# Token weights loaded in squares and turned on VectorE, all left-hand operands 32 bytes lower

## The chip, the core and the metric

The kernel runs on one core of a Trainium2 chip. The metric is the device time of one execution in microseconds (us); the median of three runs of the kernel before is 1181.59 us (1181.41 to 1181.63). TensorE is also called PE here, VectorE DVE, ScalarE ACT, GpSimd POOL, and SyncE SP.

## What is computed

Three blocks follow each other on activations of 4 sequences, 448 tokens and 768 features: sigmoid attention, a block that mixes tokens with a low-rank map and then applies a wide two-layer perceptron, and a block that mixes tokens with two full 448x448 matrices. The change touches how those two matrices (`w_tok_r`, `w_tok_i`) are brought in.

```python
attn = 1 / (1 + exp(-(q @ k.T / sqrt(64) - log(448))))     # 4 x 12 heads
x = heads_side_by_side(attn @ v)                           # 4 x 448 x 768

u  = x + (x.T @ U @ V).T                                   # rank 32
x  = u + relu(u @ w_ch1) @ w_ch2                           # 768 -> 3072 -> 768

theta = x @ w_theta
y = w_tok_r @ (x * cos(theta)) + w_tok_i @ (x * sin(theta))
u = x + y
out = u + relu(u @ w_ch)
```

The weights of the second and third block come as 64-bit floats. The kernel reads each as two 32-bit words and makes of them a rounded high part and a low part (type fp32r). A product is then three matmuls: high by high, high by low and low by high.

## The kernel before

`X` holds the activations, turned (features on the partitions), in SBUF for the whole run. PE's work comes in stages, one after the other: attention (to 163 us), the wide perceptron (163 to 883), projection by `w_theta` and mixing of tokens (883 to 1084), and the last product by `w_ch` (1084 to 1174).

**The wide perceptron.** It runs over 12 slices i of the 3072 inner features and, in each, over the 4 sequences b. `ch1(i, b)` (L674 to L676) makes 36 matmuls of 448 columns into a PSUM tile `g`: the weights are slices of `w1`, the moving operands are `uh` and `ul`, the high and low part of the sequence's activations. ACT then makes `gh` of it (L681) and DVE `gl` (L682). `ch2(i, b)` (L696 to L698) makes 36 matmuls into three PSUM tiles `y`, 12 each; the weights are slices of `w2`, the moving operands `gh` and `gl`. DVE adds each `y` to `X` (L700). The order on PE is `ch1(i, b)`, then `ch2` of the pair before it, then `ch1` of the next pair. `uh` and `ul` of the sequences 0 and 1 lie in a pool `u01` on the right side of SBUF, those of 2 and 3 in `u23` on the left.

**The mixing of tokens.** `mix` (L886 to L888) multiplies weights `zh` and `zl` (left side) by the moving operand `tok` (right side). The projection (L809 to L813) takes `xh` and `xl` (right side) as weights and `th_r` (left side, in the rings of `w1` and `w2`) as the moving operand, in 384 columns. The last stage (L967 to L969) has `wc_r` as weights and `uh`, `ul` as moving operands, all on the left.

**Bringing weights in.** Each piece of weight is a `Conv` with a list of steps: `size` (ACT), `bits`, `top` and `word` (DVE) rebuild 32-bit floats from the two words, then `finish` splits them into high and low. The load of a piece is issued in the `size` step of the piece two places before it in the queue. A table `units`, filled by `place` and `place_extra`, says at which tick (slice i, sequence b, point t) a step is taken: t = 0 is before `ch1(i, b)`, t = 1 between `ch1` and `ch2`, t = 2 to 4 behind each of the three `y` tiles of that `ch2`. The engines keep the order in which the code is written.

The seven pieces of the token weights (`conv_tok`, `tok0` to `tok6`) are made during slices i = 2, 4, 6 (two each) and i = 8 (one), spilled to DRAM as `tok_d` and loaded back together as `tok` in the last slice. They must be turned, since the token index of the sum has to lie on the partitions. Before the change a piece lies as 112 partitions by 4 x 128, and PE turns it by four transposes against an identity into a PSUM tile `tkt` (L265), in the middle of a `ch2`; ACT copies the high part from there (L110), and DVE subtracts it (L119). The pieces of `w_theta` and `w_ch` that are spilled in the same way (`conv_kept`) need no turn.

Of the kernel before, what the change touches and what calls it, by code (L numbers as in the profile page):

```python
# [11 lines left out]
F32 = mybir.dt.float32  # L12
F32R = mybir.dt.float32r
U32 = mybir.dt.uint32
# [5 lines left out]
def f(t):  # L20
    return t.bitcast(F32)
# [3 lines left out]
def tile_kernel(  # L25
# [15 lines left out]
    nc = tc.nc  # L41
    B, H, S, D = q.shape
    DM = H * D
    R = moe_U.shape[1]
    DF = moe_w_ch1.shape[1]
    P = 128
    CP = 112
    NC = S // CP
# [9 lines left out]
    NFULL = S // P  # L58
    NZ = 2 * NFULL + 1
    NS = S // R  # L60
# [22 lines left out]
    cpool = ctx.enter_context(tc.tile_pool(name="cpool", bufs=1))  # L83
# [4 lines left out]
    ident = cpool.tile([P, P], F32, name="ident")  # L88
# [10 lines left out]
    tok_w = (w_tok_r.bitcast(U32), w_tok_i.bitcast(U32))  # L99
# [9 lines left out]
    def hi_act(o, i):  # L109
        nc.scalar.activation(o, i, AF.Copy)  # L110
# [7 lines left out]
    def lo_dve(o, i, h):  # L118
        nc.vector.tensor_sub(o, i, f(h))  # L119
# [50 lines left out]
    def split(o, a, lo):  # L170
        hi_act(o[:, 0], a)
        lo(o[:, 1], a, o[:, 0])
# [66 lines left out]
    def conv_tok(i):  # L239

        n_, o_ = divmod(i, NFULL)
        st = {}

        def dma(s):
            if i < NZ - 1:
                nc.sync.dma_start(
                    out=s.rearrange("p (c s) t -> p c (s t)", c=NC),
                    in_=tok_w[n_][:, 2 * o_ * P:2 * (o_ + 1) * P].rearrange("(c p) w -> p c w", p=CP),
                )
            else:  # L250
                sv = s.rearrange("p (c a s) t -> p c a (s t)", c=NC, a=2)
                for n in range(2):
                    nc.sync.dma_start(
                        out=sv[:, :, n], in_=tok_w[n][:, 2 * NFULL * P:].rearrange("(c p) w -> p c w", p=CP)
                    )

        def dest():
            st["t"] = spill_tile(f"tok{i}")
            st["n"] = st["t"][:CP, 2 * S:2 * S + NC * P]
            return st["n"].bitcast(U32)  # L260

        def turn():
            ps = ps_g.tile([P, 2, 512], F32, tag="g", name=f"tkt_{i}", bufs=2)
            for c in range(NC):
                nc.tensor.transpose(ps[:, 0, c * CP:(c + 1) * CP], st["n"][:, c * P:(c + 1) * P], ident[:CP, :CP])  # L265
            st["o"] = st["t"][:, :2 * S].rearrange("p (a n) -> p a n", a=2)
            o = st["o"].bitcast(F32R)
            hi_act(o[:, 0], ps[:, 0, :S])
            lo_dve(o[:, 1], ps[:, 0, :S], o[:, 0])

        def spill():
            nc.sync.dma_start(out=tok_d[:, :, i, :], in_=st["o"])
        return Conv(f"tok{i}", CP, NC * P, dma, None, False, [turn, spill], dest)

    def conv_U(par):
        def dma(s):
# [94 lines left out]
    kT_t, qT_t = {}, {}  # L371
# [194 lines left out]
    nc.vector.memset(bias_s, NEG_LOG_S)  # L566
    nc.vector.memset(half_pi, math.pi / 2)
    warm = cpool.tile([P, 1], F32, name="warm")
    gate = cpool.tile([P, 1], F32, name="gate")
    load_qk(0)  # L570
    make_identity(nc, ident)
    nc.scalar.activation(warm, bias_s, AF.Sigmoid)
# [35 lines left out]
    for p in range(NP):  # L608
# [4 lines left out]
            TK(p + 1)  # L613
            TQ(p + 1)()
        if p == 0:
            nc.gpsimd.tensor_copy(gate, kT_t[1][:, :1])
            seq[0].load()
            seq[1].load()
        if p:
# [13 lines left out]
        if b >= 0 and r < NK // 2:  # L633
            ps = ps_a.tile([P, 2, 512], F32, tag="ux", name=f"h_{b}_{r}")
# [28 lines left out]
    ps_g, ps_g_st = pool("ps_g", "right", PSUM)  # L663
# [85 lines left out]
    for i in range(NB):  # L749
        for b in range(B):  # L750
# [3 lines left out]
            if i == L and b == 1:  # L754
# [3 lines left out]
                tok = tokhl.tile([P, 2, NZ, S], F32R, name="tok")  # L758
# [32 lines left out]
    ps_t, st = pool("ps_t", "right", PSUM)  # L791
    ctx.enter_context(st)
    ps_e, st = pool("ps_e", "left", PSUM)
    ctx.enter_context(st)
    zp, st = pool("zp")
# [154 lines left out]
    for bi, b in enumerate(turns_):  # L950
        for e2 in range(NK // 2):
# [3 lines left out]
            else:  # L955
                ps = ps_t.tile([P, 2, 512], F32, tag="th", name=f"wc_{b}_{e2}", bufs=2)
# [3 lines left out]
            for e in range(2):  # L960
                m = 2 * e2 + e
                o = ps1[e][:, 0, :S] if final else ps[:, e, :S]
# [42 lines left out]
```

## Time and profile before

| What | Value |
|---|---|
| median of three runs | 1181.59 us |
| the profiled execution | 1180.82 us |
| its span, first to last instruction | 1179.0 us |
| TensorE busy | 1169.3 us, 6442 matmuls |
| VectorE busy | 643.3 us |
| ScalarE busy | 360.5 us |
| GpSimd busy | 176.7 us |
| TensorE's granted clock, mean | 0.999 of 2.4 GHz |
| DMA | 100.57 MB, 85 GB/s on average |

A matmul's recorded duration is longer than the distance to the next one's start, since matmuls overlap. So the starts of matmuls are read, and the lengths of stretches cut at such starts; the durations aren't added up.

### The profile page before, as it was taken

Reading aid. Unit: us, or ns where it says so; the run is one execution under the profiler, and the core shown is the slowest. Engines: PE = TensorE matmul, PEld = TensorE weight load, DVE = VectorE, ACT = ScalarE, POOL = GpSimd, SP = SyncE. Lnnn points to the kernel's source line nnn. Section 1 sums busy time; section 2 is a strip of 40 time slices with the busy share of each in tenths; the row PEclk is TensorE's granted clock in tenths of the full one; section 3 lists DMA queues with packets and bytes.
Section 4 is the critical chain, followed back from the end, with each engine's and each line's share of the span. In section 5 each row is a group of like instructions: output and inputs, shape, how many; then the busy total and the mean of one; then the engine's idle time right before and its main releaser. Section 6 shows DMA issues by size and latency. Waiting matters only on the chain.

```text
span 1179.0 us, 15627 instructions
## 1 busy us (share of the span) xinstructions
PE 1169.3 (99%) x6442; PEld 1003.2 (85%) x6442; DVE 643.3 (55%) x805; ACT 360.5 (31%) x465; POOL 176.7 (15%) x129
## 2 busy tenths in 40 slices
PE   8999999999999999999999999999999999999998
PEld 4444468999999999999999999999999999999997
DVE  5787763455555555555545566565375543732443
ACT  6878753121212121212121212122125341620110
POOL 3200014010101010101010112122002221410000
PEclk9999999999999999999999999999999999999999
DMA  8877700113231223132313232424431000120333
GB/s 181 173 160 157 170 30 1 54 54 96 70 112 54 97 70 112 54 96 69 112 54 97 81 123 69 146 63 152 163 134 54 1 1 1 48 114 1 63 64 63
DMA packets 174439, 100.57 MB, mean 85 GB/s; under 512 B 138368, under 2 KB 165376, under 8 KB 174240
## 3 DMA queue, kind: packets, MB, share of 16 engines
q1 hardware_dynamic: 147520, 87.95, 26.2%
q0 software_dynamic: 2368, 8.24, 2.3%
q10 hardware_dynamic: 24480, 3.39, 1.7%
q8 instruction: 50, 0.82, 0.3%
q14 instruction: 21, 0.17, 0.1%
HBM read 81.40 MB, written 18.15 MB: 84 GB/s over the span
## 4 chain that ended last, share of the span: by engine, by line
PE 99%; ACT 0%; POOL 0%; issue 0%; DVE 0%; POOLq 0%
PE y L696 10%; PE g L674 10%; PE y L697 10%; PE y L698 10%; PE g L675 10%; PE g L676 10%; PE av L428 5%; PE sc L402 4%; PE y L888 3%; PE y L886 3%; PE y L887 3%; PE th L809 3%; PE th L813 3%; PE th L810 2%; PE wc L967 2%; PE wc L969 2%
## 5 line engine op out<-in xcount | busy, mean ns | idle before, releaser
L700 DVE TENSOR_TENSOR X<-y,X 128x896 f32<-128x896 f32 x144 | 157.1, 1091 | 118.8 <-PE y L698 118.7
L696 PE MATMUL y<-gh,w 128*128 128x448 f32 x576 | 212.6, 369 | 0.0
L674 PE MATMUL g<-uh,w 128*128 128x448 f32 x576 | 211.9, 368 | 0.0
L698 PE MATMUL y<-gh,w 128*128 128x448 f32 x576 | 211.8, 368 | 0.0
L697 PE MATMUL y<-gl,w 128*128 128x448 f32 x576 | 211.7, 367 | 0.0
L675 PE MATMUL g<-ul,w 128*128 128x448 f32 x576 | 211.7, 367 | 0.0
L676 PE MATMUL g<-uh,w 128*128 128x448 f32 x576 | 210.7, 366 | 0.0
L681 ACT ACTIVATE gh<-g 128x896 fp32r<-128x896 f32 x48 | 44.2, 920 | 421.5 <-PE g L676 421.5
L682 DVE SCALAR_TENSOR_TENSOR gl<-g,gh 128x896 fp32r<-128x896 f32 x48 | 52.4, 1092 | 195.6 <-ACT gh L681 195.6
L113 POOL TENSOR_TENSOR w<-ca_w,w 128x768 fp32r<-128x768 f32 x42 | 78.0, 1856 | 502.5 <-ACT w L110 502.5
L674 PEld LDWEIGHTS g<-uh,w 128*128 128x128 f32 x576 | 108.0, 187 | 11.8 <-ACT uh L110 0.7
L696 PEld LDWEIGHTS y<-gh,w 128*128 128x128 f32 x576 | 108.1, 188 | 11.4 <-issue 1.0
L698 PEld LDWEIGHTS y<-gh,w 128*128 128x128 f32 x576 | 108.1, 188 | 10.6
L697 PEld LDWEIGHTS y<-gl,w 128*128 128x128 f32 x576 | 108.2, 188 | 10.3
L676 PEld LDWEIGHTS g<-uh,w 128*128 128x128 f32 x576 | 108.2, 188 | 10.1
L675 PEld LDWEIGHTS g<-ul,w 128*128 128x128 f32 x576 | 108.1, 188 | 9.7
L393 ACT ACTIVATE A<-sc,bias_s 128x896 f32<-128x896 f32 x72 | 72.2, 1007 | 23.4 <-PE sc L402 13.2
L428 PE MATMUL av<-A,v 128*64 128x448 f32 x288 | 64.5, 556 | 0.0
L886 PE MATMUL y<-tok,zh 128*128 128x448 f32 x168 | 61.8, 368 | 0.0
L888 PE MATMUL y<-tok,zl 128*128 128x448 f32 x168 | 61.8, 368 | 0.0
L887 PE MATMUL y<-tok,zh 128*128 128x448 f32 x168 | 61.3, 365 | 0.0
L110 ACT ACTIVATE w<-ca_w 128x768 fp32r<-128x768 f32 x48 | 40.3, 840 | 65.3 <-PE y L698 64.8
(140 smaller groups left out, 1628.4 us busy)
## 6 DMA issues: line engine op xcount, KB each, us to landing
ws_w<-in_moe_w_ch_dram SPq DMA_DIRECT2D x40, 768.0 KB, 4.3
ws_w<-in_moe_w_ch_dram POOLq DMA_DIRECT2D x8, 768.0 KB, 5.9
k<-in_k_dram SPq DMA_DIRECT2D x94, 56.0 KB, 2.5
q<-in_q_dram SPq DMA_DIRECT2D x93, 56.0 KB, 2.6
ws_th<-in_moe_w_theta_dram SPq DMA_DIRECT2D x6, 768.0 KB, 4.2
th_d<-sp_th SPq DMA_DIRECT2D x6, 768.0 KB, 4.0
ws_wc<-in_moe_w_ch_dram SPq DMA_DIRECT2D x6, 768.0 KB, 4.9
wc_d<-sp_wc SPq DMA_DIRECT2D x6, 768.0 KB, 3.6
```

The source lines that it names most:

```text
L113: nc.gpsimd.tensor_sub(o, a, b)
L428: nc.tensor.matmul(ps[h * D:(h + 1) * D, :S], v_t[p // 2][:, 2 * (p % 2) + h, c, :], A_t[p, c][:, h, :], start=c == 0 and p % 2 == 0, stop ...
L674: nc.tensor.matmul(o, wh[:, sl], uh_t[b][:, kk, :], start=kk == 0, stop=False)
L675: nc.tensor.matmul(o, wh[:, sl], ul_t[b][:, kk, :], start=False, stop=False)
L676: nc.tensor.matmul(o, wl[:, sl], uh_t[b][:, kk, :], start=False, stop=kk == NK - 1)
L696: nc.tensor.matmul(o, wh[:, sl], gh[:, j, :], start=j == 0, stop=False)
L697: nc.tensor.matmul(o, wh[:, sl], gl[:, j, :], start=False, stop=False)
L698: nc.tensor.matmul(o, wl[:, sl], gh[:, j, :], start=False, stop=j == FB - 1)
L700: nc.vector.tensor_add(x, ps[:, :, :S], x)
L886: nc.tensor.matmul(o, zh[:, sl], tok_h[:, i, :], start=n == 0, stop=False)
L887: nc.tensor.matmul(o, zh[:, sl], tok_l[:, i, :], start=False, stop=False)
L888: nc.tensor.matmul(o, zl[:, sl], tok_h[:, i, :], start=False, stop=n == NZ - 1)
```

## The change

A piece is now loaded as four groups of 32 partitions, one for each group of 32 columns of the matrix, so that each 32x32 square of it lies turned in its place among the squares but not within itself: four DMAs of 32x14x64 words instead of one of 112x4x256 (for the last piece, two from each matrix instead of one from each). DVE's transpose, which works on squares of 32x32, then finishes the turn in one instruction. The piece becomes an ordinary `Conv` with a `finish` step: DVE transposes `ca` into the spill tile, ACT copies the high part, POOL subtracts. PE, the PSUM tile and DVE's subtraction drop out. With a `finish` step the table places `word` behind the last `y` of the sequence before (t = 4) and `finish` at t = 0, and the spill comes at t = 3 instead of 4.

The second edit removes the tile `gate` (128 x 1) and writes the one-column copy that paces the first loads into `warm` instead. A tile of one column takes 32 bytes of each partition. In the built programs the places are, in bytes from the start of a partition:

| Tile | Side | Before | After |
|---|---|---|---|
| `X` | left | 17088 | 17088 |
| `warm` | left | 60096 | 60096 |
| `gate` | left | 60128 | none |
| first of the `w1`/`w2` rings | left | 60160 | 60128 |
| first `gh`, first `gl` | left | 121600, 128768 | 121568, 128736 |
| `uh`, `ul` of sequence 2 | left | 135936, 146688 | 135904, 146656 |
| `uh`, `ul` of sequence 0 | right | 186336, 197088 | 186336, 197088 |
| first `xh`, first `xl` | right | 191968, 198112 | 191968, 198112 |
| `tok` | right | 204256 | 204256 |

All left tiles behind `gate` lie at multiples of 64 before and 32 bytes past one after; so do those of attention, of `z` and of the last stage. The right side isn't moved; its operands lie 32 bytes past a multiple of 64 in both. Lines of a matmul's operand are 512 or 1792 bytes long, both multiples of 64.

```diff
--- before.py
+++ after.py
@@ -239,38 +239,29 @@
     def conv_tok(i):
 
         n_, o_ = divmod(i, NFULL)
+        cols = [(n_, o_ * P + a * R) for a in range(P // R)]
+        if i == NZ - 1:
+            cols = [(a // 2, NFULL * P + a % 2 * R) for a in range(P // R)]
         st = {}
 
         def dma(s):
-            if i < NZ - 1:
+            sv = s.rearrange("p (c j) t -> p c (j t)", c=NS)
+            for a, (n, s0) in enumerate(cols):
                 nc.sync.dma_start(
-                    out=s.rearrange("p (c s) t -> p c (s t)", c=NC),
-                    in_=tok_w[n_][:, 2 * o_ * P:2 * (o_ + 1) * P].rearrange("(c p) w -> p c w", p=CP),
+                    out=sv[a * R:(a + 1) * R],
+                    in_=tok_w[n][:, 2 * s0:2 * (s0 + R)].rearrange("(c i) w -> i c w", i=R),
                 )
-            else:
-                sv = s.rearrange("p (c a s) t -> p c a (s t)", c=NC, a=2)
-                for n in range(2):
-                    nc.sync.dma_start(
-                        out=sv[:, :, n], in_=tok_w[n][:, 2 * NFULL * P:].rearrange("(c p) w -> p c w", p=CP)
-                    )
-
-        def dest():
+
+        def fin(a, t):
             st["t"] = spill_tile(f"tok{i}")
-            st["n"] = st["t"][:CP, 2 * S:2 * S + NC * P]
-            return st["n"].bitcast(U32)
-
-        def turn():
-            ps = ps_g.tile([P, 2, 512], F32, tag="g", name=f"tkt_{i}", bufs=2)
-            for c in range(NC):
-                nc.tensor.transpose(ps[:, 0, c * CP:(c + 1) * CP], st["n"][:, c * P:(c + 1) * P], ident[:CP, :CP])
+            x = st["t"][:, 2 * S:3 * S]
+            nc.vector.transpose(out=x, in_=a)
             st["o"] = st["t"][:, :2 * S].rearrange("p (a n) -> p a n", a=2)
-            o = st["o"].bitcast(F32R)
-            hi_act(o[:, 0], ps[:, 0, :S])
-            lo_dve(o[:, 1], ps[:, 0, :S], o[:, 0])
+            split(st["o"].bitcast(F32R), x, lo_pool)
 
         def spill():
             nc.sync.dma_start(out=tok_d[:, :, i, :], in_=st["o"])
-        return Conv(f"tok{i}", CP, NC * P, dma, None, False, [turn, spill], dest)
+        return Conv(f"tok{i}", P, S, dma, fin, False, [spill])
 
     def conv_U(par):
         def dma(s):
@@ -566,7 +557,6 @@
     nc.vector.memset(bias_s, NEG_LOG_S)
     nc.vector.memset(half_pi, math.pi / 2)
     warm = cpool.tile([P, 1], F32, name="warm")
-    gate = cpool.tile([P, 1], F32, name="gate")
     load_qk(0)
     make_identity(nc, ident)
     nc.scalar.activation(warm, bias_s, AF.Sigmoid)
@@ -613,7 +603,7 @@
             TK(p + 1)
             TQ(p + 1)()
         if p == 0:
-            nc.gpsimd.tensor_copy(gate, kT_t[1][:, :1])
+            nc.gpsimd.tensor_copy(warm, kT_t[1][:, :1])
             seq[0].load()
             seq[1].load()
         if p:
```

PE, in `ch2(2, 1)` around the turn of `tok0`, before:

```order
L697 MATMUL y_1_1_3200<-gl_1_3074,w_2_1_3026 128x448
L698 MATMUL y_1_1_3200<-gh_1_3073,w_2_1_3026 128x448
L265 MATMUL tkt_3214<-ident,sp_tok_3132 128x112 x4
L696 MATMUL y_1_2_3222<-gh_1_3073,w_2_0_2785 128x448
L697 MATMUL y_1_2_3222<-gl_1_3074,w_2_0_2785 128x448
```

And after, at the same place:

```order
L687 MATMUL y_1_1_3208<-gl_1_3076,w_2_1_3028 128x448
L688 MATMUL y_1_1_3208<-gh_1_3075,w_2_1_3028 128x448
L686 MATMUL y_1_2_3224<-gh_1_3075,w_2_0_2784 128x448
L687 MATMUL y_1_2_3224<-gl_1_3076,w_2_0_2784 128x448
L688 MATMUL y_1_2_3224<-gh_1_3075,w_2_0_2784 128x448
```

The four transposes are gone, and nothing stands in their place; the numbers behind the names are buffers.

DVE, from the second `y` of `ch2(2, 0)` to the second `y` of `ch2(2, 1)`, before:

```order
L700 TENSOR_TENSOR X<-y_0_1_3099,X 128x2x448
L151 SCALAR_TENSOR_TENSOR ws_tok_2936<-ca_tok_3082,ws_tok_2936 112x512
L700 TENSOR_TENSOR X<-y_0_2_3114,X 128x2x448
L157 SCALAR_TENSOR_TENSOR sp_tok_3132<-ca_tok_3082,ws_tok_2936 112x512
L147 TENSOR_SCALAR ws_w_3_0_3029<-ws_w_3_0_3029 128x768
L151 SCALAR_TENSOR_TENSOR ws_w_3_0_3029<-ca_w_3_0_3130,ws_w_3_0_3029 128x768
L157 SCALAR_TENSOR_TENSOR ca_w_3_0_3130<-ca_w_3_0_3130,ws_w_3_0_3029 128x768
L682 SCALAR_TENSOR_TENSOR gl_2_3175<-g_2_3137,gh_2_3174 128x896
L700 TENSOR_TENSOR X<-y_1_0_3185,X 128x2x448
L147 TENSOR_SCALAR ws_tok_3080<-ws_tok_3080 112x512
L700 TENSOR_TENSOR X<-y_1_1_3200,X 128x2x448
L119 TENSOR_TENSOR sp_tok_3132<-tkt_3214,sp_tok_3132 128x448
```

And after:

```order
L690 TENSOR_TENSOR X<-y_0_1_3104,X 128x2x448
L151 SCALAR_TENSOR_TENSOR ws_tok_2935<-ca_tok_3087,ws_tok_2935 128x448
L690 TENSOR_TENSOR X<-y_0_2_3119,X 128x2x448
L157 SCALAR_TENSOR_TENSOR ca_tok_3087<-ca_tok_3087,ws_tok_2935 128x448
L258 STREAM_TRANSPOSE sp_tok_3138<-ca_tok_3087 128x448
L147 TENSOR_SCALAR ws_w_3_0_3031<-ws_w_3_0_3031 128x768
L151 SCALAR_TENSOR_TENSOR ws_w_3_0_3031<-ca_w_3_0_3136,ws_w_3_0_3031 128x768
L157 SCALAR_TENSOR_TENSOR ca_w_3_0_3136<-ca_w_3_0_3136,ws_w_3_0_3031 128x768
L672 SCALAR_TENSOR_TENSOR gl_2_3183<-g_2_3145,gh_2_3182 128x896
L690 TENSOR_TENSOR X<-y_1_0_3193,X 128x2x448
L147 TENSOR_SCALAR ws_tok_3082<-ws_tok_3082 128x448
L690 TENSOR_TENSOR X<-y_1_1_3208,X 128x2x448
```

The turn stands behind the third conversion step, ahead of the next weight's conversion and of `gl`; the subtraction behind the second `y` has left DVE (it stands on POOL now).

## Rows read from the trace of the kernel before

**Rows 1.** The page: busy time of each engine; granted clock in 40 slices, in tenths.

```profile
PE 1169.3 (99%) x6442; PEld 1003.2 (85%) x6442; DVE 643.3 (55%) x805; ACT 360.5 (31%) x465; POOL 176.7 (15%) x129
...
PEclk9999999999999999999999999999999999999999
```

**Rows 2.** The view of waits, PE alone: us in total, times, longest.

```profile
PE warm L588 <- POOL ident masks.py:199: 3.4, 1, 3.4
PE sc L402 <- ACT A L393: 1.0, 2, 0.5
```

**Rows 3.** The view of windows; first column: length, from one matmul's start to another's.

```profile
core 0: us, PE busy (x) PEld busy (x) DVE busy (x) ACT busy (x) POOL busy (x), PEclk, DMA share, GB/s
163.54:173.91 10.37, 10.37 (x52) 9.56 (x51) 7.54 (x10) 4.78 (x10) 4.37 (x3) 1.00 0.01 2
221.31:228.67 7.36, 7.36 (x37) 6.75 (x36) 3.48 (x4) 0.00 (x0) 0.00 (x0) 1.00 0.30 100
250.91:258.35 7.44, 7.44 (x37) 6.76 (x36) 3.48 (x4) 0.00 (x0) 0.00 (x0) 1.00 0.33 103
258.35:265.79 7.44, 7.44 (x37) 6.76 (x36) 4.61 (x5) 3.39 (x4) 1.86 (x1) 1.00 0.01 5
683.05:690.35 7.30, 7.30 (x37) 6.76 (x36) 5.81 (x5) 0.85 (x1) 2.24 (x1) 1.00 0.64 236
697.65:705.01 7.36, 7.36 (x37) 6.75 (x36) 3.48 (x4) 0.00 (x0) 0.00 (x0) 1.00 0.31 103
876.20:883.29 7.09, 7.09 (x36) 6.57 (x35) 4.50 (x5) 0.84 (x1) 1.85 (x1) 1.00 0.27 112
883.29:889.53 6.24, 6.24 (x37) 6.24 (x36) 1.09 (x1) 0.00 (x0) 0.00 (x0) 1.00 0.81 303
944.01:953.55 9.54, 9.54 (x56) 9.50 (x55) 3.41 (x4) 1.82 (x3) 0.00 (x0) 1.00 0.01 2
1037.12:1084.44 47.32, 47.32 (x235) 43.42 (x234) 12.18 (x24) 6.14 (x11) 1.85 (x1) 1.00 0.06 23
1084.44:1091.88 7.44, 7.44 (x38) 6.76 (x37) 2.29 (x5) 0.00 (x0) 0.00 (x0) 1.00 0.01 2
```

The stretches are, in this order: the first `ch1` (b = 0), from its second matmul; `ch1(1, 0)`; `ch1(1, 2)`; `ch2(1, 1)`; `ch1(8, 3)`, behind the seventh turn; `ch1(9, 0)`; the last `ch2`, from its second matmul; two stretches of the projection; the last mixing; the first set of the last stage. A count in brackets also takes in instructions that only reach into the stretch.

**Rows 4.** The timeline of PE around the first turn: start, duration (us), instruction.

```profile
322.67 0.55 PE L265 MATMUL tkt<-ident,sp_tok 112*128 112x112 f32 x4
322.99 0.46 PE L696 MATMUL y<-gh,w 128*128 128x448 f32 x1
323.28 0.37 PE L697 MATMUL y<-gl,w 128*128 128x448 f32 x1
```

**Rows 5.** The view of windows over whole slices, i = 1, 2 and 8.

```profile
221.31:280.67 59.36, 59.36 (x289) 54.05 (x288) 31.89 (x33) 11.69 (x14) 7.42 (x4) 1.00 0.19 60
280.67:340.50 59.83, 59.83 (x297) 54.77 (x296) 32.30 (x36) 12.23 (x16) 7.43 (x4) 1.00 0.26 83
638.21:697.65 59.44, 59.44 (x294) 54.42 (x293) 33.79 (x35) 12.80 (x16) 9.67 (x5) 1.00 0.36 116
```

**Rows 6.** Groups by line and shape: busy us, mean ns of one, idle before.

```profile
L682 DVE SCALAR_TENSOR_TENSOR gl<-g,gh 128x896 fp32r<-128x896 f32 x48 | 52.4, 1092 | 195.6 <-ACT gh L681 195.6
...
L113 POOL TENSOR_TENSOR ul<-X,uh 128x448 fp32r<-128x448 f32 x15 | 17.8, 1222 | 46.5 <-ACT uh L110 46.5
...
L375 DVE STREAM_TRANSPOSE kT<-k 128x448 f32<-128x448 f32 x24 | 15.2, 632 | 5.6 <-DMA k<-in_k_dram 5.4 <-issue 0.2
...
L119 DVE TENSOR_TENSOR sp_tok<-tkt,sp_tok 128x448 fp32r<-128x448 f32 x7 | 4.3, 619 | 0.0
```

**Rows 7.** DMA issues: queue, count, KB each, median us from issue to landing.

```profile
ws_tok<-in_moe_w_tok_r_dram SPq DMA_DIRECT2D x3, 448.0 KB, 5.1
...
ws_U<-in_moe_U_dram POOLq DMA_DIRECT2D x4, 112.0 KB, 3.4
```

**Rows 8.** The instructions on tile `ws_tok`: duration (ns), first and last start (us).

```profile
L143 ACT ACTIVATE ca_tok<-ws_tok x7: 657/659/661, 304.6 to 662.1; 112x512 f32<-112x512 f32 x7
...
L246 SPq DMA_DIRECT2D ws_tok<-in_moe_w_tok_r_dram x3: 328/375/424, 279.4 to 398.5; - x3
```

## Prediction

> **What bounds the kernel now.** I read the page's busy times first. TensorE (PE) is busy for 1169.3 of the span's 1179.0 us, VectorE for 643.3, ScalarE for 360.5, and the granted clock stands at its upper level, 2.4 GHz, in every slice [rows 1]. Next the view of waits, for PE alone: it waits 3.4 us for the identity at the start and 1.0 us for ScalarE, and for nobody else [rows 2]. So no other engine's work matters unless it comes to be waited for. The time is a number of matmuls times the distance from the start of one to the start of the next, which I call the pitch. The view of windows gives the pitch: its first column is the length of a stretch that I cut from one matmul's start to a later one's, each a set of 36 matmuls of 448 columns. I shall call 36 such matmuls a set.
>
> The sets aren't equally long, although their work is [rows 3]. A `ch1` set for b = 0 or 1 takes 7.36 us (204.4 ns a matmul). One for b = 2 or 3 takes 7.44 us (206.7 ns), with the same weights. A `ch2` set takes 7.44, and so does a set of the last stage (`wc`). Behind the TensorE turn of a token piece a `ch1` set for b = 3 takes 7.30 us (202.8 ns), and the `ch1` for b = 0 that follows 7.36 again. Other engines' activity doesn't sort these: the DMA share is 0.30 in a 7.36 set, 0.33 in one 7.44 set and 0.01 in another.
>
> What does sort most of them is where the moving operand starts. `uh` and `ul` of b = 0 and 1 lie in a pool on the right side of SBUF, 32 bytes past a multiple of 64. Those of b = 2 and 3, `gh`, `gl`, and in the last stage `uh`, lie on the left, at multiples of 64. The mixing stage, whose moving operand `tok` lies on the right at such an offset too, needs 47.32 us for 231 matmuls, 204.9 ns each, where the left ones need 206.7 [rows 3]. Weights `w`, `z` and `wc` lie on the left at multiples of 64 throughout.
>
> **The turns on TensorE go.** Around the first turn the timeline has the four transposes at 322.67, the next `ch2` matmul at 322.99 and the one behind it at 323.28 [rows 4]. So four transposes and one matmul take 0.61 us; a matmul at the pace of that set would be 0.21, which leaves 0.40 us for a turn. Seven turns: 7 x 0.40 = **2.8 us** taken off PE's path.
>
> The Trainium skill ("TensorE: Matmul & The Clock Gate", section "Part 4: PE-mode transpose") gives about 275 ns for one such transpose in a kernel's context. By it, as an estimate, the 28 transposes would be 7.7 us and the sum below 4.9 us better. The trace disagrees: four of them and their after-effect are 0.40 us, because they overlap.
>
> The turns also leave the fast pace behind, and that goes with them if nothing else sets it. From the first turn of an i to the next `ch1` for b = 0 lie 84 matmuls (12 + 36 + 24 + 12; at the seventh 12 + 36 + 36), four times: 336, or 9.3 sets at 7.30. The stretches of a whole i bear this out: with two turns 59.83 us, without 59.36, with one 59.44 [rows 5]. A pair costs 0.47 net where 2 x 0.40 were spent.
>
> **What comes instead.** VectorE's three conversion steps go from 512 columns to 448. Its subtraction, 0.62 us, goes to GpSimd (the row of this shape: 1.22 us), and the turn comes to it; a turn of this shape, `kT`'s, takes 0.63 [rows 6]. So VectorE's load stays. The turn stands before the conversion of the next weight, in front of `gl`. Queued behind it is `gl`, which `ch2` needs only a set of `ch2` later; VectorE stands idle 195.6 us before the 48 `gl`, 4.1 us each on average, and that covers 0.63. If that cover were gone, each turn would cost at most its 0.63 us, 4.4 in all. The pieces of `wc` already take the same path (conversion, split over ScalarE and GpSimd, spill, with 768 columns), and PE waits for none of them. The loads become four issues of 112 KB in runs of 256 bytes instead of one of 448 KB in runs of 1 KB. The nearest rows land in 3.4 us (`U`, 112 KB) and 5.1 (the piece today) [rows 7]; the first piece is issued at 279.4 and first read at 304.6 [rows 8], so even four landings in a row, 13.6 us, are hidden. The cost of all this on PE's path is **nothing**, with 0 and 4.4 us as ends.
>
> **All left operands move 32 bytes.** After the change every left-hand tile lies where the right-hand ones already lie. The forecast is that moving operands then go at the pace of today's offset rows, 7.36 a set. There are 48 + 48 + 12 = 108 sets. 24 of them (`ch1`, b = 0 and 1) keep their 7.36. Of the other 84 about 10 run near 7.30 today (the 9.3 above, and most of the last `ch2`: 35 matmuls in 7.09 us [rows 3]) and 74 at 7.44. So 74 x 0.08 = **5.9 us** off, and 10 x 0.06 = **0.6 us** on.
>
> The trace has no matmul stream in which weights and moving operand are both offset, so this pace is bounded by neighbours. The best offset row is the first `ch1`, 10.37 us for 51 matmuls, 203.3 ns or 7.32 a set; the worst is the mixing stage, 7.375. I take 7.36, the row with the same program and most samples. For operands in other shapes: the projections (504 matmuls, moving operand on the left, weights on the right) show 6.24 us for 36 and 9.54 for 54, 173.3 and 176.7 ns, with one placement, so 1.7 us either way; the mixing stage's weights move, 504 matmuls between 204.9 and 206.7, 0.9 us either way; attention's 160 us could move by the same 1.1% as 7.44 against 7.36, 1.7 us. I take nothing for each, lacking a row for a sign, and keep them for the range.
>
> **Sum.** -2.8 - 5.9 + 0.6 = -8.1 us. On the profiled execution's 1180.82 us this is 1172.7 (its span 1179.0 becomes 1170.9). That execution was 0.8 us below the median of 1181.59, so for the median **1173.5 us**. With 7.32 to 7.375 for the pace and 2 us for the other shapes this case alone reaches from 1167 to 1177.
>
> **Rivals.** (1) The offset does nothing: what sorts b = 0 and 1 from 2 and 3 is their place, not 32 bytes. Then only the turns count: -2.8, and 9.3 sets return from 7.30 to 7.44, +1.3, in sum -1.5: 1180.1 us. For it: the 7.30 sets have aligned operands, so alignment doesn't decide alone. Against it: `tok`, in another place with the same offset, is also below 206.7.
> The Trainium skill ("SBUF — State Buffer", section "Specifications (TRN2)") names cachelines of 16 bytes as what full bandwidth depends on. By that rule a shift of 32 bytes, two whole lines, changes nothing, and this rival's result follows. The trace shows two paces between operands that differ by 32 bytes modulo 64, which speaks against it.
> (2) What counts is the offset between weights and moving operand, which differs today just in `ch1` for b = 0 and 1 and in the mix. Then all fall to 206.7: -1.5, + 24 x 0.08, + 504 x 1.8 ns, together +1.3: 1182.9 us.
> (3) With no set that pulls the pace back, everything keeps the 7.30 seen behind the turns: -2.8 - 74 x 0.14 - 24 x 0.06 = -14.6: 1167.0 us. For it: the fast pace holds for 84 matmuls until a set with another offset comes, and after the change there is none. Against it: nothing starts it.
> (4) Slower: offset weights cost in the weight loads of `ch1`, `ch2` and `wc` as much as offset moving operands save, so that the two together stand at 7.52. Then 74 x 0.08 + 24 x 0.16 + 10 x 0.22 - 2.8 = +9.2: 1190.8 us. It makes the kernel measurably slower from a mean set of 7.46 on, against 7.41 today. For it: no row has both. Against it: the projections' offset weights show no price at 173.3 ns for 384 columns.
>
> **How the numbers follow.** Forecast 0.50, (1) 0.13, (2) 0.11, (3) 0.12, (4) 0.14. A measurement of this kernel tells about 0.2%, 2.4 us, from no change; (1) and (2) lie within it. Faster: 0.50 + 0.12 = 0.62; same: 0.24; slower: 0.14. The range takes in all but (4) and the tails: from 1166.5, under (3), to 1183.2, just over (2).
>
> **What would show it.** Right: PE still waits only for the identity and ScalarE, no transposes stand in `ch2`, stretches of all i are equal, and `ch1` for b = 2 and 3, `ch2` and `wc` sets take 7.32 to 7.38 us. Sets that still take 7.44 mean (1), with b = 0 and 1 at 7.44 as well (2), sets at 7.30 (3), above 7.5 (4). A PE wait for `gl`, or idle time before the token conversion put down to a DMA, would break the step that costs the new path at nothing.

## The result, and the profile after

The changed kernel takes 1171.13 us (1170.08 to 1171.98) against 1181.50 us of the kernel before on the same chip: ratio 0.9911, with a 95% interval of 0.9898 to 0.9925, so 10.4 us faster. The forecast was 8.1. The time lies in the range and the sign is right, but that the sum comes so near is in part luck: two errors, -6.2 and +4.5 us in the profiled execution, nearly cancel. The sets became faster than forecast, and the start of the kernel became longer, which the sum does not have.

The profiled execution took 1170.08 us (10.7 less than the one of before). Cut at the first matmul of each stage, in us:

| Stretch | Before | After | Difference |
|---|---|---|---|
| to the first `ch1` | 163.23 | 167.75 | +4.52 |
| wide perceptron | 720.06 | 707.44 | -12.62 |
| projection and mixing | 201.15 | 199.69 | -1.46 |
| last stage | 89.07 | 87.35 | -1.72 |
| behind the last matmul | 5.50 | 6.06 | +0.56 |

The view of windows of the changed kernel (columns as in [rows 3]) has the stretches that answer to [rows 3] and [rows 5]: `ch1(1, 0)`, `ch1(1, 2)`, `ch2(1, 1)`, `ch1(8, 3)`; the slices i = 1 and 2; the last `ch2`, from its second matmul; the last mixing; the last stage, all of it:

```profile
225.28:232.58 7.30, 7.30 (x37) 6.76 (x36) 3.48 (x4) 0.00 (x0) 0.00 (x0) 1.00 0.30 99
254.47:261.77 7.30, 7.30 (x38) 6.76 (x37) 3.48 (x4) 0.00 (x0) 0.00 (x0) 1.00 0.29 96
261.77:269.06 7.29, 7.29 (x37) 6.76 (x36) 4.62 (x5) 3.36 (x4) 1.85 (x1) 1.00 0.04 14
677.64:684.93 7.29, 7.29 (x38) 6.76 (x36) 5.80 (x5) 0.85 (x1) 2.23 (x1) 1.00 0.50 172
225.28:283.65 58.37, 58.37 (x290) 54.10 (x288) 31.92 (x33) 11.69 (x14) 7.40 (x4) 1.00 0.18 61
283.65:342.02 58.37, 58.37 (x289) 54.10 (x288) 33.63 (x36) 12.28 (x16) 11.07 (x6) 1.00 0.38 107
867.97:875.20 7.23, 7.23 (x37) 6.57 (x36) 4.49 (x5) 0.85 (x1) 1.84 (x1) 1.00 0.29 116
1027.98:1074.88 46.90, 46.90 (x234) 43.48 (x233) 12.17 (x24) 6.27 (x11) 1.85 (x1) 1.00 0.06 25
1074.88:1162.23 87.35, 87.35 (x432) 80.96 (x431) 38.48 (x68) 8.42 (x16) 0.00 (x0) 1.00 0.42 60
```

From `ch2(0, 1)` on every set takes 7.30 us, whichever side its moving operand lies on, with DMA shares from 0.04 to 0.50. A slice that makes two token pieces is as long as one that makes none. That is rival (3), to the digit, not the forecast's 7.36. One set is an exception, the last `ch2`: behind its first matmul 35 matmuls take 7.23 us, 206.6 ns each, where the kernel before needs 7.09 for them, 202.6 each [rows 3].

TensorE's waits are no longer those of [rows 2]. The view of waits of the changed kernel, PE alone:

```profile
PE warm L578 <- POOL ident masks.py:199: 3.4, 1, 3.4
PE sl L402 <- DVE qT L354: 1.8, 1, 1.8
PE sc L393 <- ACT A L384: 1.0, 2, 0.6
PE sc L393 <- DVE ql L119: 0.5, 1, 0.5
PE sc L393 <- DVE qh L357: 0.3, 1, 0.3
PE y L686 <- DVE X L690: 0.2, 1, 0.2
```

The wait of 0.2 us for `X` stands right before the last `ch2`. Three waits for VectorE's `q` are new, 2.6 us, all in the first 30 us. VectorE in turn waits there for the loads of `q` and `k`. Its waits from 0 to 40 us, before:

```profile
DVE qT L363 <- DMA q<-in_q_dram: 6.8, 5, 2.5
DVE kT L375 <- DMA k<-in_k_dram: 4.5, 1, 4.5
```

and after:

```profile
DVE qT L354 <- DMA q<-in_q_dram: 8.8, 4, 4.9
DVE kT L366 <- DMA k<-in_k_dram: 6.2, 2, 5.7
```

The loads' order, sizes and queues are the same; they land later. The view of DMA issues (queue, count, KB, median us to landing), before:

```profile
k<-in_k_dram SPq DMA_DIRECT2D x94, 56.0 KB, 2.5
q<-in_q_dram SPq DMA_DIRECT2D x93, 56.0 KB, 2.6
...
out_dram<-o SPq DMA_DIRECT2D x48, 56.0 KB, 2.2
...
q<-in_q_dram ACTq DMA_DIRECT2D x3, 56.0 KB, 2.5
k<-in_k_dram POOLq DMA_DIRECT2D x2, 56.0 KB, 3.1
```

and after:

```profile
k<-in_k_dram SPq DMA_DIRECT2D x94, 56.0 KB, 2.7
q<-in_q_dram SPq DMA_DIRECT2D x93, 56.0 KB, 3.1
...
out_dram<-o SPq DMA_DIRECT2D x48, 56.0 KB, 2.6
...
q<-in_q_dram ACTq DMA_DIRECT2D x3, 56.0 KB, 3.2
k<-in_k_dram POOLq DMA_DIRECT2D x2, 56.0 KB, 3.9
```

The tiles of attention moved by the same 32 bytes as all left tiles. `k` and `q` are written in runs of 128 bytes, and `o`, which goes out in 2.6 us instead of 2.2, moved too. In this execution the clock fell as well. PE alone in windows of 4 us (length, PE busy, granted clock, DMA share, GB/s), before and then after:

```profile
24.00:28.00 4.00, 4.00 (x28) 1.00 0.67 109
28.00:32.00 4.00, 4.00 (x32) 1.00 0.95 188
```

```profile
24.00:28.00 4.00, 2.23 (x12) 0.90 0.72 143
28.00:32.00 4.00, 4.00 (x20) 0.67 0.70 118
```

Behind the 1.8 us in which PE stood idle the granted clock fell from its upper level (2.4 GHz) to the lower one; 0.67 is its mean over the four us from 28 on. At the matmul that the kernel before starts at 23.7 us the changed kernel is 2.96 us behind it, and at the one of 26.5 us, which it starts at 31.0, it is 4.5 behind: the difference of 1.6 grew while the clock was low. From there on both need 136.7 us to the first `ch1`, so attention's pace is unchanged, and in this execution the whole loss lies ahead of it. The idle time alone doesn't bring the clock down: e11 below stands idle at the same place for the same 1.8 us, and its clock stays up:

```profile
24.00:28.00 4.00, 2.21 (x12) 1.00 0.57 104
28.00:32.00 4.00, 4.00 (x30) 1.00 0.70 117
```

### The profile page after: what moved, and what is told of

The parts are those of the page before. It is cut to its first block, busy times and chain, and to the rows that moved or that the text cites. A ratio compares the mean times of both kernels' runs of the same rounds, so it can differ in the third digit from the quotient of the medians.

```text
span 1168.3 us, 15638 instructions
## 1 busy us (share of the span) xinstructions
PE 1155.3 (99%) x6414; PEld 1000.5 (86%) x6414; DVE 647.9 (55%) x805; ACT 360.9 (31%) x465; POOL 189.5 (16%) x136
## 4 chain that ended last, share of the span: by engine, by line
PE 97%; DMA 1%; SPq 1%; DVE 1%; ACT 0%; issue 0%; ACTq 0%
PE g L664 10%; PE g L666 10%; PE g L665 10%; PE y L686 10%; PE y L688 10%; PE y L687 10%; PE av L419 5%; PE sc L393 4%; PE y L877 3%; PE y L876 3%; PE y L878 3%; PE th L799 3%; PE th L803 3%; PE th L800 2%; PE wc L958 2%; PE wc L959 2%
## 5 line engine op out<-in xcount | busy, mean ns | idle before, releaser
L113 POOL TENSOR_TENSOR zl<-t,zh 128x768 fp32r<-128x768 f32 x23 | 42.7, 1880 | 115.4 <-ACT zh L110 115.4
```

Source lines behind the costliest of these rows:

```text
L113: nc.gpsimd.tensor_sub(o, a, b)
```

## The experiments

I give places as the start of a line modulo 256 bytes. Left is that of `w`, `gh`, `z` and so on, right that of `uh` of b = 0 and 1 and of `tok`; the distance is right minus left. Before: left 0, right -32, distance -32. After: both -32, distance 0. In every kernel the weights and moving operands of `ch2`, of `ch1` for b = 2 and 3 and of the last stage lie on the left at distance 0; only `ch1` for b = 0 and 1, the projection and the mixing cross the sides. No kernel leaves any work out. Summary, with lengths read from the profiled executions:

| Kernel | Left, right | Distance | Attention at | First `ch1` at | `ch1` b = 0, 1 | `ch2` | Perceptron | Last stage | Median us | Ratio, 95% interval |
|---|---|---|---|---|---|---|---|---|---|---|
| before | 0, -32 | -32 | 0 | 163.23 | 7.36 | 7.44 | 720.06 | 89.07 | 1181.5 | 1 |
| after | -32, -32 | 0 | -32 | 167.75 | 7.30 | 7.30 | 707.44 | 87.35 | 1171.13 | 0.9911 [0.9898, 0.9925] |
| e1 (after) | -32, -32 | 0 | -32 | 168.19 | 7.30 | 7.30 | 707.44 | 87.35 | 1170.62 | 0.9908 [0.9893, 0.9923] |
| e10 (after) | -32, -32 | 0 | -32 | 168.26 | 7.30 | 7.30 | 707.43 | 87.35 | 1170.42 | 0.9903 [0.9886, 0.9919] |
| e2 squares only | 0, -32 | -32 | 0 | 165.02 | 7.36 | 7.44 | 718.76 | 89.07 | 1180.17 | 0.9991 [0.9982, 1.0001] |
| e3 shift only | -32, -32 | 0 | -32 | 168.86 | 7.30, 7.44 | 7.30, 7.44 | 714.20 | 87.35 | 1177.36 | 0.9962 [0.9949, 0.9975] |
| e4 | 0, -64 | -64 | 0 | 164.71 | 7.28 | 7.44 | 716.89 | 87.35 | 1175.01 | 0.9946 [0.9931, 0.9961] |
| e5 | 0, 128 | 128 | 0 | 163.80 | 7.34 | 7.30, 7.43 | 709.57 | 87.35 | 1171.42 | 0.9908 [0.9893, 0.9923] |
| e6 (turns on PE) | 0, 128 | 128 | 0 | 163.95 | 7.34 | 7.30, 7.43 | 712.23 | 87.34 | 1173.84 | 0.9931 [0.9915, 0.9948] |
| e7 | -32, -32 | 0 | 0 | 166.83 | 7.30 | 7.30 | 707.36 | 87.35 | 1167.87 | 0.9880 [0.9865, 0.9894] |
| e8 | -32, -64 | -32 | -32 | 168.74 | 7.36 | 7.44 | 718.61 | 89.07 | 1183.39 | 1.0011 [1.0002, 1.0020] |
| e9 | 0, 0 | 0 | 0 | 163.87 | 7.30 | 7.30 | 707.44 | 89.07 | 1167.91 | 0.9883 [0.9868, 0.9897] |
| e11 | 0, 0 | 0 | 64 | 167.05 | 7.30 | 7.30 | 707.43 | 87.35 | 1170.52 | 0.9905 [0.9890, 0.9920] |
| e12 | 0, 0 | 0 | 0 | 163.96 | 7.30 | 7.30 | 707.43 | 87.35 | 1166.58 | 0.9874 [0.9858, 0.9891] |

Each ratio is against the kernel before on the same chip (1181.3 to 1182.0 us).

**The changed kernel again (e1).**

> The changed kernel once more, to see whether the 4.5 us that its first 31 us lost against the kernel before come back. Theory A (the loss belongs to the change, as attention's tiles too lie 32 bytes lower): the first ch1 starts at 167 to 168 us again, and the time is 1170 to 1172 us. Theory B (the loss came from outside, DMA packets of 128 bytes that took up to 354 ns in that execution): the first ch1 starts near 163 us and the time is 1166 to 1168 us. Both expect sets of 7.30 us in ch1, ch2 and the last stage.

1170.62 us, with the first `ch1` at 168.19 and `q` landing in 3.3 us. The loss at the start is the kernel's, not that execution's. The fall of the clock is not: in e1, and in e10, the same kernel once more, the granted clock stays at 1.00 throughout attention. These two have lost 2.9 and 3.0 us at the matmul that the kernel before starts at 26.5 us, and lose two more between its 40 and 56 us. There e2, whose attention tiles lie where they were, loses 1.6 us too, so this second part isn't shown to come from the shift.

**The parts alone (e2, e3).** Against the changed kernel, e2 is

```diff
+    gate = cpool.tile([P, 1], F32, name="gate")
...
-            nc.gpsimd.tensor_copy(warm, kT_t[1][:, :1])
+            nc.gpsimd.tensor_copy(gate, kT_t[1][:, :1])
```

and e3 is the kernel before with the opposite edit.

> The squares and VectorE's turn alone; the tile gate is kept, so that left-hand operands lie at multiples of 64 and right-hand ones 32 bytes past one, as before. Every theory of the pace expects that ch1 sets for b = 0 and 1 stay at 7.36 us, all others at 7.44, and that no set is at 7.30, since the turns that started the fast pace are gone: 1.5 us under the kernel before, 1180.0 us. If the squares themselves brought the faster pace, it would be about 1167 to 1171 us. If the new path held up TensorE, waits for gl or X would show and the time would be above 1181.5 us.

> The kernel before with the tile gate removed alone: turns stay on TensorE, left-hand operands move 32 bytes. Theory M (a moving operand at an odd multiple of 32 is fast by itself) and theory H (a matmul set keeps the pace it comes in with, as long as its operands have the same offset as those before it) both expect 7.30 us a set; the turns cost 7 x 0.40 = 2.8 us, so the time is 2.8 us over the changed kernel's on the same chip. If squares and shift only work together, sets stay at 7.36 and 7.44 and the time at 1181.5 us.

The squares alone give what rival (1) had for them: 1180.17 us, and no set at 7.30. (The ratio's interval takes in 1; it is the perceptron, 718.76 us against 720.06, that shows the gain.) Without the turns nothing brings the fast pace in e2; with distance -32 in `ch1` for b = 0 and 1 the rest stays at 7.44. The shift alone was expected 2.8 us behind the changed kernel and came out 6.7 behind. The view of windows of e3 shows why; the stretches are the 24 matmuls ahead of the third turn, the `ch1` set behind it, the one behind the fourth, a `ch1` set ahead of the seventh, the one behind that, and the following `ch1(9, 0)`:

```profile
438.70:443.57 4.87, 4.87 (x26) 4.47 (x25) 2.52 (x3) 2.21 (x3) 1.85 (x1) 1.00 0.17 71
446.44:453.88 7.44, 7.44 (x37) 6.76 (x36) 4.18 (x5) 0.00 (x0) 0.00 (x0) 1.00 0.49 167
461.66:468.95 7.29, 7.29 (x37) 6.76 (x36) 3.48 (x4) 0.00 (x0) 0.00 (x0) 1.00 0.77 277
667.02:674.32 7.30, 7.30 (x38) 6.76 (x37) 4.08 (x5) 0.00 (x0) 0.00 (x0) 1.00 0.57 190
682.05:689.49 7.44, 7.44 (x37) 6.76 (x36) 5.80 (x5) 0.85 (x1) 2.23 (x1) 1.00 0.66 237
696.93:704.37 7.44, 7.44 (x37) 6.76 (x36) 3.48 (x4) 0.00 (x0) 0.00 (x0) 1.00 0.28 97
```

The same product at the same places runs at 7.30 or at 7.44. The pace holds from set to set; the first two turns leave it at 7.30, the third takes it to 7.44, the fourth back, the fifth and sixth do the same, and the seventh takes it to 7.44 again, where it stays up to the last `ch2`, `ch1` for b = 0 and 1 included. So at distance 0 there are two lasting paces, and a disturbance can switch between them, in either direction. In the kernel before, the first turn of each pair and the seventh switched to the fast one, and the next set at distance -32 switched back. A turn isn't needed: ahead of the last `ch2` PE's stream stops in every kernel (one matmul starts 0.41 to 0.56 us behind the other instead of 0.21), and behind that stop the set goes from slow to fast in the kernel before, e3 and e8 and from fast to slow in the changed kernel, e7, e9 and e12.

**What the place is measured by (e4, e5, e6).** e4 moves the right side by 32 bytes more, so that all places are multiples of 64; e5 and e6 by 96, so that all are multiples of 128. e4 and e5 have the squares and keep `gate`, e6 is the kernel before. The edit (24 words instead of 1 in e5 and e6):

```diff
+    padr, padr_st = pool("padr", "right")
+    ctx.enter_context(padr_st)
+    padr.tile([P, 1], F32, name="pad_r")
```

> Squares, gate kept, and one column of 32 bytes taken off the right side: every operand, left and right, lies at a multiple of 64. Theory M expects all 108 sets at 7.44 us, that is 24 x 0.08 = 1.9 us more than the squares alone, about 1181.9 us. Theory H expects one pace for all sets, the one they come in with: 7.30 us as in the changed kernel (1167 to 1171 us), or 7.44 throughout, but never 7.36 for b = 0 and 1 beside 7.44 for the rest. A time under 1172 us would refute M; 1181 to 1183 us leaves both.

> Squares, gate kept, 96 bytes taken off the right side: every operand, left and right, lies at a multiple of 128. The earlier run with multiples of 64 had left 128 x n and right 128 x n + 64, and its sets for b = 0 and 1 took 7.28 us beside 7.44 for the rest. Theory H2 (with the same place modulo 128 a set keeps the pace it comes in with, 7.30 or 7.44; a set whose moving operand has another place than its weights runs at a pace of its own and hands on the slow one) expects b = 0 and 1 to be no different from 2 and 3: either all sets at 7.30 (about 1167 us) or all at 7.44 (about 1181 us). Theory M2 (a moving operand at a multiple of 128 is slow) expects 7.44 in all 108 sets, about 1181.5 us. Attention's tiles lie at multiples of 64, so the first ch1 starts at 163 to 165 us under both.

> The kernel before, turns on TensorE and gate kept, with 96 bytes taken off the right side: all operands at multiples of 128. H2: a turn may change the pace, and nothing but a turn does; behind a turn that brings 7.30 the sets for b = 0 and 1 of the next slice keep 7.30 until the next turn, where the kernel before had 7.36 and then 7.44. M2: behind each turn the pace falls back to 7.44 at the next set for b = 0, as before. The time is between 1170 us (fast from the first turn on) and 1184 us (slow throughout, with 2.8 us for the turns).

Neither 64 nor 128 is the measure, and neither of the two theories of e4 or of e5 expected the sets that came. With distance -64 `ch1(1, 0)` takes 7.28 us and the `ch2` set behind it 7.44, so equal offsets modulo 64 don't make sets equal. From the view of windows of e4:

```profile
222.84:230.12 7.28, 7.28 (x38) 6.75 (x37) 3.48 (x4) 0.00 (x0) 0.00 (x0) 1.00 0.29 100
230.11:237.55 7.44, 7.44 (x37) 6.76 (x36) 3.27 (x3) 1.34 (x2) 0.00 (x0) 1.00 0.03 10
```

With distance 128 `ch1(1, 0)` takes 7.34, so it still differs from its neighbours, but from i = 2 on only the `ch2` behind it is pulled to 7.43, and the rest keeps 7.30. e6 differs from e5 only in how the pieces are turned, and the turns leave the pace alone there but for the set behind `ch1(9, 0)`, 7.31 instead of 7.43 us. The seven `ch2` sets with a turn in them are 0.39 to 0.41 us longer in e6, 2.78 in sum: these are the turns by themselves. With the 0.12 of that one set the perceptrons differ by 2.66 us, 712.23 against 709.57.

**The distance or the place (e8, e9).** e8 is the changed kernel with the right side moved by 32 bytes too, so that everything is shifted and the distance is -32 as before. e9 has `gate` and a right pad of 56 words: nothing on the left is shifted, and the distance is 0.

> The changed kernel with 32 bytes taken off the right side: left operands at 128 x n + 96, right ones at 128 x n + 64. H2 expects b = 0 and 1 (weights and moving operand 32 bytes apart modulo 128) at a pace of their own, between 7.27 and 7.40 us, and the other sets at 7.44, since each b = 1 hands on the slow pace: 1176 to 1182 us. If the left offset alone makes the pace, all sets of ch2 and of b = 2 and 3 stay at 7.30 and the time is 1170 to 1172 us.

> Squares, gate kept, 224 bytes taken off the right side: every operand, left and right, lies at a multiple of 256. So far the pattern of the sets followed the distance between right and left places modulo 256: 32 below (before, squares alone, and left odd with right even) gives 7.36 for b = 0 and 1 and 7.44 for the rest, 64 below 7.28 and 7.44, 128 off 7.34 and mostly 7.30, 0 (the changed kernel) 7.30 throughout. Theory D (only that distance counts, not the offset of 32 bytes itself) expects the changed kernel's pattern, set for set: 7.30 throughout, the mixing stage at 206.5 and 203.0 ns, the last stage at 202.7; the loads at the start and the stores at the end run as in the kernel before, so the first ch1 starts at 163 to 165.5 us: 1165 to 1168 us. Theory O (the offset of 32 bytes of the left-hand operands itself brings the pace) expects sets of 7.44 us and 1180 to 1182 us.

The shift of the left side without the distance brings nothing: the sets of e8 are those of e2, 7.36 and 7.44, and it ends at 1183.39 us, beyond the 1176 to 1182 expected and slower than before, by the loss at the start. The distance without the shift brings the whole gain in the perceptron, 707.44 us. Counted in full, the distances of the changed kernel and of e9 differ by 256 bytes, and their sets are the same. `ch1(1, 0)` and the `ch2` behind it, e8:

```profile
226.82:234.18 7.36, 7.36 (x38) 6.75 (x36) 3.48 (x4) 0.00 (x0) 0.00 (x0) 1.00 0.29 99
234.18:241.62 7.44, 7.44 (x38) 6.76 (x36) 3.27 (x3) 1.34 (x2) 0.00 (x0) 1.00 0.03 10
```

The same in e9, and then its last mixing (231 matmuls) and last stage:

```profile
221.40:228.70 7.30, 7.30 (x38) 6.76 (x37) 3.48 (x4) 0.00 (x0) 0.00 (x0) 1.00 0.27 100
228.70:235.99 7.29, 7.29 (x37) 6.76 (x36) 3.27 (x3) 1.33 (x2) 0.00 (x0) 1.00 0.03 10
1024.35:1072.16 47.81, 47.81 (x234) 43.45 (x233) 12.17 (x24) 6.25 (x11) 1.86 (x1) 1.00 0.06 23
1072.16:1161.24 89.08, 89.08 (x433) 80.91 (x431) 38.47 (x68) 8.37 (x16) 0.00 (x0) 1.00 0.37 60
```

One part of the expectation failed: the last mixing took 207.0 ns a matmul instead of 203.0 and handed the slow pace to the last stage, 89.08 us instead of 87.35.

**The loss at the start (e7, e10, e11).** e7 puts attention's tiles at multiples of 256 again in the changed kernel; e10 is the changed kernel beside e9 and e11 on one chip; e11 moves attention's tiles by 64 bytes in e9. The edit of e7 (16 words in e11):

```diff
+    ap.tile([P, 1], F32, name="pad_a")
```

> The changed kernel with one column of 32 bytes put at the start of attention's first pool, which is closed before most of the perceptron: attention's tiles (k, q, v and their parts) lie at multiples of 128 again, everything else as in the changed kernel. If the loads into tiles 32 bytes off cost the first 50 us their 4.5 to 5 us, the first ch1 starts at 163 to 165.5 us instead of 168, and the time is 2.5 to 4.5 us under the changed kernel's, 1166 to 1168 us, with sets at 7.30. If the loss came from elsewhere, the first ch1 starts at 168 us and the time is 1170 to 1171 us. The entry into the perceptron could take the other pace; then sets take 7.44 and the time is about 1182 us.

> The changed kernel on the same chip, to compare with the run at multiples of 256: 1170 to 1172 us, first ch1 at 167.5 to 168.5 us, sets at 7.30 us. If theory D and the account of the start hold, it is 3 to 5 us slower than that run; under theory O it is 10 us faster.

> As the run at multiples of 256, with attention's tiles alone moved up by 64 bytes, so that every second run of 128 bytes that a load of k or q writes lies across a multiple of 256, as it does with the 32 bytes of the changed kernel. If it is the crossing that slows these loads, the first ch1 starts at 167 to 169 us, q lands in 3.1 us or more, and the time is 3 to 5 us above that run. If only places off a multiple of 64 are slow, the first ch1 starts at 163 to 165.5 us, q lands in 2.4 to 2.7 us, and the time is that run's.

e7 is faster than the changed kernel, but its profiled execution, the slowest of its four, reaches the first `ch1` at 166.83 us, short of what was expected. Its `q` lands in 2.6 us again and its `o` still goes out in 2.6. e11 takes 1170.52 us, level with e10 (both 2.5 to 2.6 us above e9, where 3 to 5 were expected), and reaches the first `ch1` 3.2 us later than e9: 64 bytes are about as bad as 32. Its expectation had the landing times at 3.1 and more; over all pairs `k` and `q` stood at 2.7. What moved are the first loads, on which the start hangs. From the view of DMA issues, e9 and then e11:

```profile
q<-in_q_dram ACTq DMA_DIRECT2D x3, 56.0 KB, 2.5
k<-in_k_dram POOLq DMA_DIRECT2D x2, 56.0 KB, 3.1
```

```profile
q<-in_q_dram ACTq DMA_DIRECT2D x3, 56.0 KB, 3.1
k<-in_k_dram POOLq DMA_DIRECT2D x2, 56.0 KB, 3.9
```

This pair of rows sorts all fourteen profiles by where attention's tiles lie: 2.5 to 2.7 and 3.0 to 3.2 us with them at multiples of 256, 3.1 to 3.3 and 3.8 to 3.9 with them 32 bytes below or 64 above one. How far PE falls behind goes with it, but for e7: at the matmul that the kernel before starts at 23.7 us, the six executions with attention's tiles off a multiple of 256 are 2.85 to 4.03 us behind it, the others 0.26 at most, and e7 2.03. In both of these layouts some of the 128-byte runs into `k` and `q` cross a multiple of 256, and before none does. The trace's records of 128-byte packets from 5 to 10 us show a tail only then: 13 ns is the 99th percentile and the maximum before, in e7 and in e9, but 135 and 354 ns after, 70 and 362 ns in e11. The Trainium skill ("DMA: Bandwidth & Descriptors", section "How a descriptor splits into AXI transactions") says that a transaction starts at an address aligned to 256 bytes and that bytes ahead of an unaligned start cost beats. It says so of reads, and here the writes cross; the trace agrees in direction, and no run shows the beats. In the kernel before every second run starts 128 bytes past a multiple of 256 and shows no tail, so here it isn't the unaligned start alone.

**The last mixing (e12).** e9 with the order of z products that the first two mixings have:

```diff
-    mix(2, lambda d: d == 0 and zmul(NTC - 1))
+    mix(2, lambda d: d == 1 and zmul(NTC - 1))
```

> The kernel of e9 (squares, gate kept, all operands at the same place modulo 256) with one edit: the last mix defers its last z product to the second column group instead of the first, the order that the first two mixes already have. Nothing is left out. In e9 the last mix's remaining sets ran at 207.0 ns a product and the last stage at 206.7, while the first two mixes came out of the same transposes at the quicker pace. Theory P (which of the two paces follows is decided anew where a stretch of products starts again after other work, by the order there): the last mix then takes 203.0 ns and hands it to the last stage, 202.7 ns; 89.07 becomes 87.35 us there, and the whole is about 2.5 us under e9, 1165 to 1166 us. Theory Q (the order there has no part in it; the pace falls by something else that e9 and this kernel share): 207.0 and 206.7 again, and 1168 us as in e9. Both expect the first 1792-column stage to start at 163.9 us and the 1792-column stages to last 707.4 us.

1166.58 us. The last mixing's remaining 210 matmuls and the last stage, from the view of windows of e12:

```profile
1028.80:1071.44 42.64, 42.64 (x213) 39.53 (x212) 11.54 (x23) 5.91 (x10) 1.85 (x1) 1.00 0.00 1
1071.44:1158.79 87.35, 87.35 (x432) 80.96 (x431) 38.46 (x68) 8.37 (x16) 0.00 (x0) 1.00 0.38 61
```

203.1 ns a matmul and the fast last stage, as theory P expected. The median is 1.3 us under e9's, which the intervals of the two ratios don't tell apart; the profiled executions differ by 2.45 us, 1.72 of them in the last stage. That the order decides isn't shown by it: e11 has e9's order and came out fast too. The best kernel of the study is this one, some 4 us under the changed one by the medians (its interval, 0.9858 to 0.9891, lies below 0.9898 to 0.9925 and 0.9893 to 0.9923 of two series of that one, and overlaps the third, 0.9886 to 0.9919, at its edge).

## Why the prediction was right, and where it was not

**What bounds the kernel: right.** TensorE is busy in 99% of the span after as before, and the whole gain is pitch and turns.

**The turns, 2.8 us: right.** e6 against e5 gives 2.78. That the fast pace behind the turns goes with them was right too: e2 has no 7.30 set, and its net gain in the perceptron, 1.30 us, is rival (1)'s 1.5.

**What comes instead, nothing: right.** PE waits 0.2 us for `X`, once, and never for `gl`. VectorE's busy time went from 643.3 to 647.9 us and GpSimd's from 176.7 to 189.5; seven subtractions of 1.83 us, where the nearest row had said 1.22, are most of the latter, and nobody waits for them. This row and the turn's 0.65 us come from the groups of the changed kernel:

```profile
L113 POOL TENSOR_TENSOR sp_tok<-sp_tok 128x448 fp32r<-128x448 f32 x7 | 12.8, 1830 | 46.9 <-ACT sp_tok L110 46.9
L258 DVE STREAM_TRANSPOSE sp_tok<-ca_tok 128x448 f32<-128x448 f32 x7 | 4.5, 646 | 0.4
```

**The pace, 74 x 0.08: wrong.** This is the step that failed. I read from the rows of b = 0 and 1 that an offset moving operand runs at 7.36, and carried it to operands that are all offset. But those rows have an operand on either side, 32 bytes apart; the changed kernel has none such. What counts is the distance, which was rival (2)'s idea, but (2) looked only at where unequal places were good and took 7.44 for the price of equal ones. The rows that answer this stood in the prediction, in rival (3): 7.30 lasts from a turn "until a set with another offset comes". A distance of 0 permits both 7.30 and 7.44, and the set at another distance was what put 7.44 back. Against (3) I held that nothing starts the fast pace. It needs no turn to start: in the changed kernel `ch2(0, 1)`, at 203.40 us and close behind the small products of the low-rank map, is already at 7.29. A row of the prediction showed as much: the last `ch2` of the kernel before, 35 matmuls in 7.09 us, is fast with no turn for the three slices before it. (3) gave -14.6; the perceptron and the last stage together measure -14.34, which without the turns' 2.8 is 11.5 us where the forecast had 5.3. Its chance had been put at 0.12 beside 0.50 for the forecast.

The rule weighed against rival (1), of the Trainium skill ("SBUF — State Buffer", section "Specifications (TRN2)"), speaks of cachelines of 16 bytes. Distances of 0, -32, -64 and 128 are all whole lines, and `ch1` for b = 0 runs at 7.30, 7.36, 7.28 and 7.34 with them: the measurement differs from what the rule alone would give.

**Attention at nothing, 1.7 us either way: wrong.** Its pace didn't change, as taken, but the term left out that the shift moves the destinations of its loads as well. It measured +4.52 us in the profiled execution: 2.6 of new waits, and most of the rest while the clock was low behind one of them. In e1 and e10 the loss is 5.0 without the fall of the clock, so that part of the account holds for the one execution alone. Kernels whose attention tiles lie at multiples of 256 reach the first `ch1` between 163.2 and 165.0 us (e7: 166.8), the others between 167.0 and 168.9. The rows on landing times that I read were those of the token pieces [rows 7]; I left out those of `q` and `k`, for which VectorE already waited 6.8 and 4.5 us in the first 40.

**Projection and mixing, 2.6 us either way: right**, at -1.46. The tail's +0.56, with `o` going out 0.4 us later, was not priced.

Put together: -8.1, then -6.2 for the pace, +4.5 for the start, -1.5 for the middle, +0.6 for the tail, is -10.7, the measured difference of the profiled executions.

**Open.** Why the distance modulo 256 sets the pace, and what in a disturbance picks one of the two paces at distance 0, no run tells. e9 and e11 run the same products at the same places, and their last stages differ by 1.7 us. Of the changed kernel three profiled executions show the fast pace in the perceptron, but for its last set, and in the last stage; whether other executions switch isn't known. Nor is settled why e7 recovers so little of the start in its profiled execution, when e9, with all left tiles in the old places, recovers all of it; the staging tiles of the weights and `o` are 32 bytes low in e7 still, and no run moves them alone.

## What to carry to other kernels

Where TensorE is the bound, read the pitch set by set, and where equal work has two pitches compare the places of both operands with each other, not each with a power of two; here one tile of one column on one side was worth 11.3 us in one stage (e2 against the changed kernel, 718.76 and 707.44). Before moving everything by a few bytes, look at which DMAs write into the moved tiles and who waits for them first: padding the other side (e9) brought the same pace and left the loads alone. A pace that persists past its cause belongs to a history, so look also for the step that resets it.

## What was unexpected in the hardware

- 36 matmuls of 448 columns in this type take 7.28, 7.34 or 7.36 us with operands at distances of -64, 128 and -32 bytes modulo 256, and 7.30 or 7.44 at a distance of 0.
- At distance 0 there are two paces, 202.7 and 206.7 ns a matmul; each lasts for tens of sets, and four transposes of 112 columns (e3), or a stop of PE's stream of 0.2 to 0.35 us (ahead of the last `ch2`), can switch from either to the other.
- A tile 32 or 64 bytes off a multiple of 256 makes the first loads of `q`, in runs of 128 bytes, land in 3.1 to 3.3 us instead of 2.5 to 2.7, and those of `k` in 3.8 to 3.9 instead of 3.0 to 3.2.
- The same 1.8 us of idle PE at 24 us were followed by a fall of the granted clock (mean 0.67 from 28 to 32 us) in the changed kernel's profiled execution, and by none in e11.
